# Early operand splits for the output projection, and twelve attention stages on other ticks

## The chip, the core and the metric

One core of one Trainium2 chip runs the whole program. The metric is the device time of one execution in microseconds. The kernel before took 687.49 us (median of three executions, from 686.54 to 687.96). The profiled execution took 686.53 us; its span from the first to the last instruction is 684.8 us. The clock that was granted to TensorE was 1.00 of full speed in the whole span.

The engines are called as in the profile: PE is TensorE's matmul, PEld its weight load, DVE is VectorE, ACT is ScalarE, POOL is GpSimd, SP is SyncE, which here only issues DMAs.

## What is computed

A layer normalisation feeds an attention with a compressive memory and a gated feed-forward network (FFN); both results are added to x. S is 2048, D is 448, there are 16 heads of 28 and 4 segments of 512 tokens, F is 1792.

```
xn = layernorm(x)
for each segment s of 512 tokens:                  # q, k, v = xn @ wq, xn @ wk, xn @ wv
    p = softmax(qs @ ks.T * scale + causal mask)   # within the segment, 16 heads
    a_dot = p @ vs
    a_mem = phi(qs) @ M / (phi(qs) @ z + 1e-6)     # M, z: sums over the earlier segments
    o[s] = g * a_mem + (1 - g) * a_dot
    M, z = M + phi(ks).T @ vs, z + sum(phi(ks))
out = x + o @ wo + (sigmoid(xn @ w_gate) * (xn @ w_up)) @ w_down
```

All matmul operands that need float32 accuracy are split in a high and a low part, and a product is made of eleven matmuls (the list `TERMS`): high by high, high by low and low by high.

## The kernel before

**Stages.** A front part (about the first 150 us) normalises x, and makes values, keys, queries and the memory's share, which goes to the DRAM tensors `od`. Then comes one long part with an order written out by hand, in which three streams of work are mixed; each engine works through its own instructions in the order in which the program gives them out.

1. The FFN (`gated`). For each of 7 pairs of feature tiles and each of 4 blocks of 512 tokens it makes two gate products and two up products of 11 matmuls each (line 254), and between them the down products of the block before, 6 matmuls each (line 180). ACT takes a tanh of a gate product (line 261), DVE multiplies it with the up product (line 271), ACT copies the result to `hh` (line 277), DVE makes its low part (line 280), and DVE adds each down product to `acc` (line 182). A block is 20 steps (`yield`s).
2. The attention within segments (`attention`). A `Pair` is two heads of a segment, a `Unit` two pairs, called A (even) and B (odd) here. There are 16 units.
3. The output projection (`project`): for each of 16 tiles of 128 tokens, `split_tokens` makes the high part of the attention's output in `xs` on ACT (line 802) and the low part on DVE (lines 109 and 110), and 11 matmuls (line 820) multiply it with the output weights. It begins when the FFN's generator is through; its first matmuls stand behind the splits of tiles 0, 1 and 2.

**Ticks.** The attention's work is put on a list of ticks, 28 to a unit (`TICKS`). After each step of the FFN or of the projection the main loop gives out as many ticks as are due, 473 ticks over 541 steps, so about 0.87 of a tick to a step. 28 ticks are 32 steps, so the units lie in five different ways on the FFN's blocks of 20 steps, and every fifth unit lies in the same way. Within a tick the work goes by rank: scores (0), exponents and the unit's sums (1), loads (2), maxima (3), joins (4), subtractions (5), the work behind a unit (6).

A pair goes through these stages; the tables give the tick of each, counted from the unit's first:

- `SCORES`, `score(k)`, five steps: PE makes a block of transposed scores (line 638) in one of two PSUM banks, ACT copies it to `w` (lines 642 and 645), POOL masks the diagonal (line 653). Step 0 takes a new buffer `w` of three; that buffer was the result's buffer of the unit two before, which a DMA of the POOL queue stores (line 740). After the last step SP issues the six loads of the pair after the next.
- `MAXIMA`, `maximum(k)`, three steps on DVE (lines 660 and 664): each needs the masked scores.
- `JOINS`, `join(k)`: step 0 is three small DVE maxima (lines 673 to 675) and a copy on POOL (678); step 1 is one DVE maximum (680) and a POOL copy (681); step 2 is one DVE maximum (683) and two POOL copies (684, 685); step 3 is a DVE transpose that spreads the maxima to `mb` (688).
- `SUBTRACT`, `subtract(k)`, three steps on DVE (line 702), and `EXPONENTS`, `exponents(k)`, three on ACT (line 706).
- At tick 28 + 15 `finish` makes the unit's sums (line 724) on PE out of the exponentials of both pairs.
- `BEHIND`: `back` (a DVE transpose out of PSUM, line 730), `divide` (142, 143), `turn` (736), and `store`, the DMA on the POOL queue.

PSUM has 8 banks: two for scores, two for up products, two shared by gate and down products, one for down products, one for the unit's sums. So a matmul waits for the DVE or ACT instruction that empties its bank, and `finish` for the exponentials.

`load_sums(0)` and `load_sums(1)` read the attention's output of the first two blocks back from DRAM; they are issued behind the last scores of pairs 30 and 31, at ticks 435 and 446.

Of the kernel before, what the change touches and what calls it, by code (L numbers as in the profile page):

```python
# [11 lines left out]
AF = mybir.ActivationFunctionType  # L12
# [4 lines left out]
P = 128  # L17
# [19 lines left out]


TICKS = 28
SCORES = ((2, 4, 7, 10, 15), (16, 20, 21, 24, 26))  # L40
MAXIMA = ((10, 13, 16), (23, 26, 28))
JOINS = ((17, 18, 19, 20), (29, 30, 31, 33))
SUBTRACT = ((22, 25, 26), (33, 34, 37))
EXPONENTS = ((25, 27, 31), (34, 36, 39))
BEHIND = (17, 18, 19, 24)
SUMS, END = 15, 25


# [20 lines left out]
def kernel(  # L69
# [11 lines left out]
    V, A, G, T = nc.vector, nc.scalar, nc.gpsimd, nc.tensor  # L81
# [6 lines left out]
    xs = [keep.tile([P, 7, L], F32R, name=f"xs{b}") for b in range(NB)]  # L88
# [18 lines left out]
    def transpose_low(p3, dst, t):  # L107
        tok = slice(t * P, (t + 1) * P)
        V.tensor_sub(dst[:, 4:7, tok], p3[:, 0:3], dst[:, 0:3, tok].bitcast(F32))
        V.tensor_sub(dst[64:, 3, tok], p3[64:, 3], dst[64:, 3, tok].bitcast(F32))  # L110
# [11 lines left out]
    def bank(name, tag):  # L122
        return ps.tile([P, L], F32, name=name, tag=tag, bufs=banks[tag])
# [177 lines left out]
    with tc.tile_pool(name="front", bufs=2) as sb, tc.manual_schedule(engines=FRONT):  # L301
# [227 lines left out]
        for b in range(NB):  # L529
# [24 lines left out]
            for k, c in enumerate((3, 4, 5, 6, 0, 1, 2) if last else range(7)):  # L554
# [34 lines left out]
                n = k - 1 if b == 0 else k + 1  # L589
# [152 lines left out]
    pairs = [Pair(n) for n in range(NB * H // 2)]  # L742
    units = [Unit(u, pairs[2 * u:2 * u + 2]) for u in range(NB * NG)]

    def attention():
        for n in range(2):
            pairs[n].load()
        units[0].load_values()
        yield
        plan = [[] for _ in range(n_att + 1)]  # L750

        def at(tick, rank, work, *args):
            plan[tick].append((rank, work, args))

        def following(n):
            if n < len(pairs):
                pairs[n].load()
            else:
                load_sums(n - len(pairs))

        for n, pair in enumerate(pairs):
            first = TICKS * (n // 2)
            ticks = [first + tick for tick in SCORES[n % 2]]
            for k, tick in enumerate(ticks):
                at(tick, 0, pair.score, k)
            at(ticks[-1], 2, following, n + 2)
            for k in range(3):
                at(first + MAXIMA[n % 2][k], 3, pair.maximum, k + 2)
                at(first + SUBTRACT[n % 2][k], 5, pair.subtract, k)
                at(first + EXPONENTS[n % 2][k], 1, pair.exponents, k)  # L770
            for k in range(4):
                at(first + JOINS[n % 2][k], 4, pair.join, k)
        for u, unit in enumerate(units):
            first = TICKS * (u + 1)
            at(first + SUMS, 1, unit.finish)
            if u + 1 < len(units):
                at(first + SUMS, 2, units[u + 1].load_values)
            for tick, work in zip(BEHIND, (unit.back, unit.divide, unit.turn, unit.store)):
                at(first + tick, 6, work)
        for work in plan:  # L780
            for _, run, args in sorted(work, key=lambda w: w[0]):
                run(*args)
            yield

    sums = {}

    def load_sums(b):

        if b < 2:
            sums[b] = sb.tile([P, HG, L], F32, name="sums", tag="qk2", bufs=2)  # L790
        else:
            sums[b] = sums[b - 2]
        o3 = od[b].rearrange("(h c) n -> h c n", c=32)
        for m in range(8):
            a, c = m % 2, 4 * min(m, 6)
            nc.sync.dma_start(sums[b][64 * a:64 * a + 64, m // 2, :], o3[:, c:c + 4, :])

    def project():

        def split_tokens(b, t):  # L800
            o3 = sums[b][:, :, t * P:(t + 1) * P]
            A.activation(xs[b][:, 0:4, t * P:(t + 1) * P], o3, AF.Copy)
            transpose_low(o3, xs[b], t)

        def out_weights(w):
            at = 2 * D * (w // 4) + D * (w % 2)
            return wo[w % 4 // 2][:, at:at + D]

        yield
        for n in range(NB * NT + 2):  # L810
            if n < NB * NT:
                b, t = divmod(n, NT)
                split_tokens(b, t)
                if t == NT - 1 and b + 2 < NB:
                    load_sums(b + 2)
            if n >= 2:
                b, t = divmod(n - 2, NT)
                po = bank("po", ("p", "gu")[n % 2])
                for m, (a, w) in enumerate(TERMS):
                    T.matmul(po[:, :D], xs[b][:, a, t * P:(t + 1) * P], out_weights(w),  # L820
                             start=m == 0, stop=m == len(TERMS) - 1)
                    if m in (3, 7):
                        yield
                halves = 2 if n == NB * NT + 1 else 1
                for i in range(halves):
                    part = slice(D // halves * i, D // halves * (i + 1))
                    V.tensor_add(acc[b][:, t, part], po[:, part], acc[b][:, t, part])
                    queue = nc.scalar if i else nc.sync
                    queue.dma_start(out[b * L + t * P:b * L + (t + 1) * P, part], acc[b][:, t, part])
                yield  # L830
                if rest:
                    yield from rest.pop(0)

    N_OUT = 1 + NB * NT * 3 + 12
    steps = attention()
    n_att = len(units) * TICKS + END
    done = 0
    with tc.manual_schedule(engines=MANUAL):
        next(steps)
        k = sum(FILLS) + 6  # L840
        for part in (ffn, project()):
            for _ in part:
                want = min(round(n_att * (k - LEAD) / (N_FFN + N_OUT - LEAD - TAIL)), n_att)
                k += 1
                while done < want:
                    next(steps)
                    done += 1
# [39 lines left out]
```

## Time and profile before

The program's parts in the profile, from the page's groups of instructions:

| group | instructions | busy us | mean ns |
|---|---|---|---|
| down products, PE line 180 | 672 | 155.3 | 366 |
| scores, PE line 638 | 256 | 62.0 | 314 |
| unit's sums, PE line 724 | 512 | 37.8 | 436 |
| output projection, PE line 820 | 176 | 36.7 | 364 |
| subtractions, DVE line 702 | 96 | 100.7 | 1055 |
| maxima, DVE line 660 | 64 | 79.0 | 1234 |
| additions of down products, DVE line 182 | 112 | 67.6 | 603 |
| exponentials, ACT line 706 | 96 | 87.9 | 916 |
| masks, POOL line 653 | 160 | 76.0 | 478 |

| | us |
|---|---|
| median of three executions | 687.49 |
| profiled execution | 686.53 |
| its span | 684.8 |

How to read the rows. A row of the timeline has the start (us from the span's start), the busy time, the engine, the line, the operation, out<-in, the shape, the number of instructions merged in it, and in brackets the time for which the engine sat idle before it with what ended that. A row of the waits has who waited for whom, the time in all, how often, and the longest. Matmuls overlap each other and their ends are modelled, so the starts tell more than the busy times.

### The profile page before, as it was taken

Reading aid. Unit: us, or ns where it says so; the run is one execution under the profiler, and the core shown is the slowest. Engines: PE = TensorE matmul, PEld = TensorE weight load, DVE = VectorE, ACT = ScalarE, POOL = GpSimd, SP = SyncE. Lnnn points to the kernel's source line nnn. Section 1 sums busy time; section 2 is a strip of 40 time slices with the busy share of each in tenths; the row PEclk is TensorE's granted clock in tenths of the full one; section 3 lists DMA queues with packets and bytes.
Section 4 is the critical chain, followed back from the end, with each engine's and each line's share of the span. In section 5 each row is a group of like instructions: output and inputs, shape, how many; then the busy total and the mean of one; then the engine's idle time right before and its main releaser. Section 6 shows DMA issues by size and latency. Waiting matters only on the chain.

```text
span 684.8 us, 10503 instructions
## 1 busy us (share of the span) xinstructions
PE 678.9 (99%) x3594; PEld 567.8 (83%) x3594; DVE 570.8 (83%) x995; ACT 338.6 (49%) x563; POOL 141.6 (21%) x349
## 2 busy tenths in 40 slices
PE   8999999999999999999999999999999999999998
PEld 7898878778878788887888878888787887888797
DVE  6765695766799899999999899899998998999754
ACT  5837555343364445645456455455544554544320
POOL 3500010101212232232212213132122231321000
PEclk9999999999999999999999999999999999999999
DMA  7446556696224331252324442324352332423352
GB/s 268 182 151 234 203 208 243 245 335 184 71 73 99 95 100 58 58 154 61 96 56 101 96 113 60 100 57 105 85 111 69 97 74 72 106 71 85 82 168 104
DMA packets 45940, 84.37 MB, mean 123 GB/s; under 512 B 6336, under 2 KB 20544, under 8 KB 45376
## 3 DMA queue, kind: packets, MB, share of 16 engines
q1 hardware_dynamic: 42736, 76.26, 37.0%
q0 software_dynamic: 3008, 7.34, 5.0%
q8 instruction: 28, 0.46, 0.3%
q14 instruction: 24, 0.20, 0.1%
q10 hardware_dynamic: 144, 0.11, 0.0%
HBM read 51.05 MB, written 32.64 MB: 122 GB/s over the span
## 4 chain that ended last, share of the span: by engine, by line
PE 89%; DVE 7%; issue 2%; POOL 1%; ACT 1%; DMA 0%; DVEq 0%; ACTq 0%; POOLq 0%
PE pgu L254 37%; PE pd L180 18%; PE pp L380 10%; PE st L638 5%; PE po L820 5%; PE pa L724 5%; PE pv L360 5%; PE pmm L408 2%; PE n L426 2%; DVE w L702 1%; DVE mx L660 1%; PE pt L102 1%; PE pk L400 1%; DVE acc L182 1%; DVE sg L271 0%
## 5 line engine op out<-in xcount | busy, mean ns | idle before, releaser
L254 PE MATMUL pgu<-xs,wgu 128*128 128x512 f32 x1232 | 302.6, 393 | 0.0
L254 PEld LDWEIGHTS pgu<-xs,wgu 128*128 128x128 f32 x1232 | 229.1, 188 | 46.2 <-issue 2.0
L180 PE MATMUL pd<-wdn,hh 128*128 128x448 f32 x672 | 155.3, 366 | 0.0
L180 PEld LDWEIGHTS pd<-wdn,hh 128*128 128x128 f32 x672 | 122.8, 188 | 11.5 <-issue 0.8
L653 POOL TENSOR_SCALAR_AFFINE_SELECT w<-w 128x256 f32<-128x256 f32 (+1 forms) x160 | 76.0, 478 | 231.2 <-ACT w L642 162.8
L706 ACT ACTIVATE w<-w 128x1024 f32<-128x1024 f32 (+1 forms) x96 | 87.9, 916 | 58.0 <-DVE w L702 58.0
L642 ACT ACTIVATE w<-st 128x512 f32<-128x512 f32 x128 | 75.7, 592 | 61.5 <-PE st L638 55.9
L702 DVE TENSOR_TENSOR w<-w,mb 128x1024 f32<-128x1024 f32 (+1 forms) x96 | 100.7, 1055 | 0.8
L660 DVE TRANSPOSE_TENSOR_REDUCE mx<-w 128x32 f32<-128x1024 f32 x64 | 79.0, 1234 | 6.6 <-POOL w L653 6.5
L380 PE MATMUL pp<-xs,wqk 128*128 128x512 f32 x308 | 77.7, 402 | 0.0
L182 DVE TENSOR_TENSOR acc<-pd,acc 128x448 f32<-128x448 f32 x112 | 67.6, 603 | 5.5 <-PE pd L180 5.5
L277 ACT ACTIVATE hh<-sg 128x512 fp32r<-128x512 f32 x56 | 35.4, 631 | 67.3 <-DVE sg L271 45.6
L380 PEld LDWEIGHTS pp<-xs,wqk 128*128 128x128 f32 x308 | 56.8, 188 | 13.4 <-issue 2.4
L638 PE MATMUL st<-qk 84*128 84x128 f32 (+3 forms) x256 | 62.0, 314 | 0.0
L261 ACT ACTIVATE sg<-pgu 128x512 f32<-128x512 f32 x56 | 33.2, 593 | 50.7 <-PE pgu L254 48.8
L638 PEld LDWEIGHTS st<-qk 84*128 84x128 f32 x256 | 47.9, 189 | 8.7 <-issue 1.4
L271 DVE SCALAR_TENSOR_TENSOR sg<-sg,pgu 128x512 f32<-128x512 f32 x56 | 37.8, 674 | 10.8 <-PE pgu L254 10.8
L387 DVE TENSOR_TENSOR qk<-pp,qk 128x512 fp32r<-128x512 f32 x28 | 19.3, 689 | 29.8 <-ACT e L385 23.7
L688 DVE STREAM_TRANSPOSE mb<-top 128x1024 f32<-128x1024 f32 x32 | 39.5, 1235 | 3.3 <-POOL top L685 3.2
L360 PE MATMUL pv<-wv,xs 128*128 128x448 f32 x176 | 39.6, 376 | 0.3 <-POOL wv L457 0.2
L280 DVE SCALAR_TENSOR_TENSOR hh<-sg,hh 128x512 fp32r<-128x512 f32 x56 | 38.2, 682 | 0.9 <-ACT hh L277 0.9
L724 PE MATMUL pa<-w,vv 128*32 128x128 f32 (+3 forms) x512 | 37.8, 436 | 0.0
(100 smaller groups left out, 638.5 us busy)
## 6 DMA issues: line engine op xcount, KB each, us to landing
qk<-qd SPq DMA_DIRECT2D x192, 112.0 KB
qd<-qk SPq DMA_DIRECT2D x28, 512.0 KB
raw<-in_w_ffn SPq DMA_DIRECT2D x14, 512.0 KB
vd<-vst SPq DMA_DIRECT2D x4, 1024.0 KB
vv<-vd SPq DMA_DIRECT2D x16, 256.0 KB
od<-w POOLq DMA_DIRECT2D x16, 256.0 KB, 4.2
sums<-od SPq DMA_DIRECT2D x32, 128.0 KB
out<-acc SPq DMA_DIRECT2D x15, 224.0 KB
```

The costliest lines, as they stand in the source:

```text
L180: T.matmul(pd[:, :D], l, r, start=n == 0, stop=n == len(mms) - 1)
L182: V.tensor_add(acc[b][:, t, :], pd[:, :D], acc[b][:, t, :])
L254: T.matmul(dst, wgu[f][:, w, side * P:(side + 1) * P], xs[b][:, a, :], start=n == 0, stop=n == len(TERMS) - 1)
L360: T.matmul(pv[:, :D], xs[b][:, a, t * P:(t + 1) * P], wv[w], start=n == 0, stop=n == len(TERMS) - 1)
L380: T.matmul(pp, wqk[c][:, w, :], xs[b][:, a, :], start=n == 0, stop=n == len(TERMS) - 1)
L638: T.matmul(st[:, at:at + L - kb * P], self.qk[:KS, 1, h, kb * P:(kb + 1) * P], self.qk[:KS, 0, h, kb * P:], start=True, stop=True)
L642: A.activation(w, st, AF.Copy)
L653: G.affine_select(d, d, pattern=pattern, base=0, channel_multiplier=-1, compare_op=ALU.is_ge, fill=MASK)
L660: V.tensor_reduce(self.mx[:, 32 * h:32 * h + 32], w3[:, h, :2 * L].rearrange("p (b n) -> p b n", n=32), axis=mybir.AxisListType.X, op=ALU. ...
L702: V.tensor_sub(w, w, m)
L706: A.activation(w, w, AF.Exp, scale=SCALE)
L724: T.matmul(pa[32 * j:32 * j + 32, kb * P:], self.vv[:, kb, 32 * j:32 * j + 32], self.pairs[j // 2].block(j % 2, kb), start=kb == 0, stop=k ...
```

## The change

Twelve entries of the tables get another tick, all but one of them a stage of pair A or of the work behind a unit. In pair A the first score moves from tick 2 to 0, the second maximum from 13 to 14 and the third from 16 to 17, the joins from 17, 18, 19, 20 to 18, 19, 20, 22, the last subtraction from 26 to 29 (tick 1 of the next unit) and the last exponential from 31 to 33 (tick 5). In pair B the first score moves from 16 to 17. Behind a unit, `divide` moves from 18 to 19 and `turn` from 19 to 20. `split_tokens` for tiles 0 and 1 of block 0 is given out at ticks 458 and 460, with rank 7, and no longer at the start of `project`.

```diff
-SCORES = ((2, 4, 7, 10, 15), (16, 20, 21, 24, 26))
-MAXIMA = ((10, 13, 16), (23, 26, 28))
-JOINS = ((17, 18, 19, 20), (29, 30, 31, 33))
-SUBTRACT = ((22, 25, 26), (33, 34, 37))
-EXPONENTS = ((25, 27, 31), (34, 36, 39))
-BEHIND = (17, 18, 19, 24)
+SCORES = ((0, 4, 7, 10, 15), (17, 20, 21, 24, 26))
+MAXIMA = ((10, 14, 17), (23, 26, 28))
+JOINS = ((18, 19, 20, 22), (29, 30, 31, 33))
+SUBTRACT = ((22, 25, 29), (33, 34, 37))
+EXPONENTS = ((25, 27, 33), (34, 36, 39))
+BEHIND = (17, 19, 20, 24)
+EARLY_SPLITS = (10, 12)
...
+    def split_tokens(b, t):
+        o3 = sums[b][:, :, t * P:(t + 1) * P]
+        A.activation(xs[b][:, 0:4, t * P:(t + 1) * P], o3, AF.Copy)
+        transpose_low(o3, xs[b], t)
...
+        for t in range(2):
+            at(TICKS * len(units) + EARLY_SPLITS[t], 7, split_tokens, 0, t)
...
-                split_tokens(b, t)
+                if n > 1:
+                    split_tokens(b, t)
```

The same function `split_tokens` stood in `project` before; it is moved so that both can call it.

More of the change, by code (lines that the diff above doesn't have):

```diff
@@ L798, in project @@
     def project():
[L800 to L803, printed above, removed]
         def out_weights(w):
```

## The prediction

> **What bounds the kernel now.** I read the page's totals first, then its two largest groups, then who waited for whom on the matmul engine and on DVE.
>
> ```profile
> span 684.8 us, 10503 instructions
> ...
> PE 678.9 (99%) x3594; PEld 567.8 (83%) x3594; DVE 570.8 (83%) x995; ACT 338.6 (49%) x563; POOL 141.6 (21%) x349
> ...
> DVE  6765695766799899999999899899998998999754
> ...
> L254 PE MATMUL pgu<-xs,wgu 128*128 128x512 f32 x1232 | 302.6, 393 | 0.0
> L254 PEld LDWEIGHTS pgu<-xs,wgu 128*128 128x128 f32 x1232 | 229.1, 188 | 46.2 <-issue 2.0
> ```
>
> ```profile
> PE po L820 <- DVE xs L109: 0.7, 1, 0.7
> ...
> PEld po L820 <- DVE xs L109: 1.0, 1, 1.0
> ...
> PEld st L638 <- ACT w L642: 0.4, 1, 0.4
> ...
> DVE sg L271 <- PE pgu L254: 10.8, 9, 2.7
> ...
> DVE mx L680 <- POOL up L678: 7.9, 11, 2.5
> DVE mx L660 <- POOL w L653: 6.5, 8, 2.3
> ...
> ACT w L642 <- DMA od<-w: 5.4, 3, 2.6
> ```
>
> PE is busy in 99% of the span. A busy PE alone proves little, since ends are modelled; but from about 155 us on the only waits of PE or PEld for another engine of over 0.2 us are the two quoted: the projection's matmul for DVE's split, once, and a score for ACT's copy, once. So TensorE sets the time, and the change can win those two waits and no more: about one microsecond. DVE is the second engine: in the attention's part nearly every slice has a 9, and what idle time it has (10.8, 7.9 and 6.5 us in the quoted waits, over 16 units) is about 1.6 us a unit. It runs some microseconds behind PE, and PE does not feel that as long as the results that it needs are early enough. The question is what twelve moved stages do to that lead.
>
> **Part 1, the early splits.** The place is where the unit's sums end and the projection begins.
>
> ```profile
> 632.32 0.69 DVE L702 TENSOR_TENSOR w<-w,mb 128x512 f32<-128x512 f32 x1
> ...
> 633.10 0.64 ACT L706 ACTIVATE w<-w 128x512 f32<-128x512 f32 x1 [0.37 <-DVE w L702]
> ...
> 635.50 2.36 PE L724 MATMUL pa<-w,vv 128*32 128x512 f32 x32
> ...
> 636.87 4.26 ACT L802 ACTIVATE xs<-sums 128x512 fp32r<-128x512 f32 x8
> ...
> 637.79 0.68 PE L820 MATMUL po<-wo,xs 128*128 128x448 f32 x2
> ...
> 638.57 0.52 DVE L109 TENSOR_TENSOR xs<-sums,xs 128x384 fp32r<-128x384 f32 x1
> 639.11 0.29 DVE L110 TENSOR_TENSOR xs<-sums,xs 64x128 fp32r<-64x128 f32 x1
> 639.13 1.71 PEld L820 LDWEIGHTS po<-wo,xs 128*128 128x128 f32 x9 [1.05 <-DVE xs L109]
> 639.13 2.08 PE L820 MATMUL po<-wo,xs 128*128 128x448 f32 x9 [0.67 <-DVE xs L109]
> ```
>
> The first two matmuls need only the high part; the third, with the low part, stands until DVE's line 109 is done at 639.09. PE's modelled idle time is 0.67 us, that of the weight loads 1.05; I take 0.85, between them. From the third matmul on there is no wait to the end, so this comes off the end in full.
>
> With the change the two splits are given out at ticks 458 and 460, before the unit's sums (tick 463). On ACT they cost 4.26 / 8 = 0.53 us each, on DVE 0.52 + 0.29 = 0.81 each. On ACT the first stands ahead of the last exponential (633.10) and delays it by at most 0.53 us, to about 634.3; the sums begin at 635.50, so over a microsecond of cover is left. On DVE they take 1.6 us of a stretch after the last subtraction, in which it idles for a part; what is queued behind them there (the split of the second half of the output weights, an FFN product, `back`) has its matmuls after 639. The third split stays where it is and its tile comes two tiles later. The work is moved, not added: the cost is 0, or 0.5 us if that cover were gone.
>
> **Part 2, the score at tick 0.** PE's score and ACT's copy of it come two ticks earlier, about 2 us (473 ticks over some 485 us). The copy still has to wait for the buffer that the store frees (the 5.4 us of ACT in the quoted waits), so ACT will stand at that place for up to 2 us longer. Behind it in ACT's queue stand an `hh` copy or a tanh, and in POOL's queue, behind the mask, the copy of B's join 0. The loads of its operands were issued 13 ticks before instead of 15. It ends the one wait of a score for a copy: 0.44 us on PEld at most, 0 if the store is as late as the copy; I take 0.2.
>
> **Part 3, the maximum at tick 17 and the joins.** This is where I expect the loss. Every fifth unit lies in the same way on the FFN's steps; I show one, and take the two others of its kind to be like it.
>
> ```profile
> 552.02 1.48 PE L180 MATMUL pd<-wdn,hh 128*128 128x448 f32 x6
> 552.29 1.23 DVE L660 TRANSPOSE_TENSOR_REDUCE mx<-w 128x32 f32<-128x1024 f32 x1
> ...
> 553.53 0.62 DVE L182 TENSOR_TENSOR acc<-pd,acc 128x448 f32<-128x448 f32 x1
> 553.57 2.67 PE L254 MATMUL pgu<-xs,wgu 128*128 128x512 f32 x11
> ...
> 554.08 0.17 DVE L673 TENSOR_TENSOR mx<-mx 128x24 f32<-128x24 f32 x1
> ...
> 554.48 0.18 DVE L675 TENSOR_TENSOR mx<-mx 128x16 f32<-128x16 f32 x1
> ...
> 554.58 0.71 DVE L730 STREAM_TRANSPOSE w<-pa 128x512 f32<-128x512 f32 x1
> ...
> 556.27 0.69 DVE L271 SCALAR_TENSOR_TENSOR sg<-sg,pgu 128x512 f32<-128x512 f32 x1 [0.98 <-PE pgu L254]
> ...
> 556.88 0.18 DVE L680 TENSOR_TENSOR mx<-mx,up 64x32 f32<-64x32 f32 x1
> ```
>
> ```profile
> 540.90 0.18 DVE L680 TENSOR_TENSOR mx<-mx,up 64x32 f32<-64x32 f32 x1 [0.37 <-POOL up L678]
> ```
>
> Line 271 waits for the up product, whose end PE sets. Before, DVE did the maximum, join 0 and `back` ahead of it, and join 1 could follow at once, since POOL had its copy done. By the ticks the order becomes: addition, maximum, `back`, line 271, join 0, join 1. So join 0 (554.08 to 554.66, 0.58 us) falls behind the wait, and join 1 then waits for POOL with nothing between, 0.37 us as at 540.90. DVE comes out 0.95 us later; 0.58 if the copy is hidden. After that it works without a pause worth the name up to these rows:
>
> ```profile
> 575.67 0.62 DVE L182 TENSOR_TENSOR acc<-pd,acc 128x448 f32<-128x448 f32 x1
> ...
> 576.83 1.37 PE L180 MATMUL pd<-wdn,hh 128*128 128x448 f32 x6
> ...
> 578.10 0.63 ACT L706 ACTIVATE w<-w 128x512 f32<-128x512 f32 x1
> ...
> 578.36 2.36 PE L724 MATMUL pa<-w,vv 128*32 128x512 f32 x32
> ...
> 579.25 0.13 PEld L724 LDWEIGHTS pa<-w,vv 128*32 128x32 f32 x4 [0.30 <-issue]
> ```
>
> The down product at 576.83 needs the bank that line 182 empties by 576.29: 0.54 us of lead, against 0.58 to 0.95 us of delay, so PE stands for 0.04 to 0.41 us. Then the last exponential, which ends at 578.73, feeds the sums' second block, which begins near 579.25: some 0.4 us of lead are left, and the delay takes 0 to 0.15 more. That is 0.04 to 0.55 a unit; I take 0.4, near the upper end, since no row shows the copy hidden when nothing stands between. Three units: 1.2 us.
>
> ```profile
> 292.43 1.22 DVE L660 TRANSPOSE_TENSOR_REDUCE mx<-w 128x32 f32<-128x1024 f32 x1
> 295.17 0.69 DVE L271 SCALAR_TENSOR_TENSOR sg<-sg,pgu 128x512 f32<-128x512 f32 x1 [1.53 <-PE pgu L254]
> ```
>
> Once more, in the unit at 292, the maximum itself changes places with line 271: 1.22 us of work goes behind a wait of 1.53 us, and with join 1's 0.37 DVE is 1.6 us late there. What lead the next sums have I bound by 0.4 us from the rows above and the whole 1.6 us: a loss of 0 to 1.2, taken at 0.4, because half a unit of DVE's waits lies between and can absorb some.
>
> ```profile
> 608.09 0.63 ACT L706 ACTIVATE w<-w 128x512 f32<-128x512 f32 x1
> ...
> 608.18 1.07 PE L724 MATMUL pa<-w,vv 128*32 128x512 f32 x8
> ```
>
> In the units at 436 and 580 the maximum already stood behind line 271, and only join 1's 0.37 us is new. At the sums that follow the exponential ends at 608.72, 0.54 us after they began; by the distance of 0.89 us to the second block (578.36 to 579.25) 0.35 us of lead are left, less a weight load of 0.13. So 0 to 0.2 a unit; I take 0.15, 0.3 for both.
>
> **Part 4, the rest.** A's last subtraction goes between B's joins 0 and 1 and fills the 0.37 us for which DVE waited there: 0 to 0.37 gained on DVE, which PE feels only where a lead is short; counted 0. The last exponential at tick 33 has a lead of ten ticks to the sums; B's first score, a tick later, has three ticks to the score that needs its bank; `divide` and `turn` come a tick later, four ticks ahead of the store: 0, and if ACT's queue is late there, some 0.1 each time.
>
> **The sum.** 686.53 - 0.85 - 0.2 + 1.2 + 0.4 + 0.3 = 687.38 us against the profiled execution, +0.85 us. That execution is the fastest that is shown, 0.96 us below the median; on the median the same step gives 687.49 + 0.85 = 688.34, said as **688.3 us**. A measurement of this kernel can tell about 0.2% (1.37 us) from no change, so this is no change that can be told.
>
> **Rivals.**
>
> *DVE has no lead to give (slower).* If the delays at tick 17 pass to PE whole, because DVE's idle places of about 1.6 us a unit are used up and one unit's delay reaches the next, the three units cost 0.95 each, the one at 292 1.6, the two others 0.37 each, and a late store under the score at tick 0 some 0.3 once: 5.5 us. With the gains of 1.05 that is +4.4 at most; half of the excess over my sum gives the likely size, +2.6: 690.1 us. It decides from the point where the delay is larger than the leads of 0.2 to 0.54 us that the rows show. For it: those leads are short. Against: the subtraction in the joins' gap gives back up to 0.37 a unit.
>
> *Only the gains.* The moved stages cost PE nothing: 687.49 - 1.05 = 686.4 us. For it: DVE's waits on POOL (7.9 and 6.5 us) are at just the stages that now get more room. Against: the order above, in which work goes behind a wait.
>
> *PE has room that its busy time hides (faster).* ACT's 5.4 us behind the store may be felt by PE under the modelled ends; if a quarter of it went with the moves, 1.4 us, the time would be 687.49 - 1.05 - 1.4 = 685.0. Against: eleven matmuls with 2.67 us from first start to last end (553.57) are as even as their loads. The Trainium skill speaks for it: Perfetto Trace Analysis, Identifying the Most-Contended Engine, says that matmul busy time misleads and that weight-load busy time tells the distance to the limit, which here is 83%. The trace does not agree that this is room: a load takes 188 ns, the wait behind it is not for another engine, and 46.2 us of PEld's idle time at line 254 has 2.0 us with a named end.
>
> *The early splits are not early*, since the third matmul then waits for something else, say the split of the output weights that they delay: part 1 is worth 0, and the sum 689.2.
>
> **Chances.** My sum 0.40, DVE without a lead 0.38, only the gains 0.12, hidden room 0.06, splits not early 0.04. Of the first, 0.34 lies within 0.2%, 0.04 above and 0.02 below; of the gains alone 0.08 within and 0.04 below; the slower rival lies above but for 0.02; the last is half and half. That makes faster 0.12, the same 0.46, slower 0.42. The range goes from the gains alone to a little past the slower rival: 686.3 to 690.5.
>
> **What would show it.** Right: the third matmul of line 820 follows the second without a wait on line 109; no score waits for line 642; DVE's join 0 stands behind line 271 at the places like 556, and a down product or the sums get a short wait for DVE or ACT about 15 to 20 us later. Wrong: PE's waits for other engines in the attention stay nil (then only the gains count), or they appear in most units (then the first rival). The forecast as a whole is wrong below 686.1 or above 688.9, 0.2% from the median.

## The result, and the profile after

| kernel | median us | lowest to highest | ratio to before, 95% interval |
|---|---|---|---|
| before | 687.05 | 686.54 to 687.96 (7 runs) | |
| changed | 689.49 | 687.93 to 690.79 (7 runs) | 1.0033 (1.0023 to 1.0043) |

The change makes the kernel 2.44 us slower, 0.33%, a little more than the 0.2% that a measurement can tell. The spread is twice as wide as well, 2.9 us against 1.4. The profiled execution of the changed kernel took 690.79 us, the longest of the seven, and that of before 686.53, the shortest, so the two traces differ by 4.26 us, more than the medians do. Which part of that is steady has to come from the experiments.

From the page of the changed kernel, the span and the engines' totals:

```profile
span 689.0 us, 10521 instructions
...
PE 679.0 (99%) x3594; PEld 566.2 (82%) x3594; DVE 570.0 (83%) x995; ACT 339.1 (49%) x563; POOL 153.8 (22%) x349
```

No engine is busy for over 0.5 us longer than before but GpSimd (141.6 before), and PE is again busy for 99%. The 4.2 us are in the waits. From the view of who waited for whom (us in total, times, longest):

```profile
ACT w L643 <- DMA od<-w: 18.7, 10, 4.7
...
PE st L639 <- ACT w L643: 2.3, 2, 1.3
PE pd L181 <- DVE acc L183: 1.7, 3, 0.6
```

The line numbers of the attention and the FFN are one higher than before (line 182 is now 183, 638 is 639, 642 is 643). The wait of the projection for DVE's split is gone. Two kinds of wait of PE are new: three down products wait for DVE's addition, and two scores for ACT's copy; ACT in turn waits for the store's DMA, 18.7 us where it was 5.4.

What each wait costs shows better in the distance between the starts of neighbouring groups of matmuls than in PE's modelled idle time. PE's rows of the timeline, before:

```profile
394.51 2.67 PE L254 MATMUL pgu<-xs,wgu 128*128 128x512 f32 x11
397.21 0.51 PE L638 MATMUL st<-qk 84*128 84x256 f32 x2
...
538.93 2.68 PE L254 MATMUL pgu<-xs,wgu 128*128 128x512 f32 x11
541.45 0.40 PE L638 MATMUL st<-qk 84*128 84x256 f32 x2
...
574.24 2.75 PE L254 MATMUL pgu<-xs,wgu 128*128 128x512 f32 x11
```

and after:

```profile
285.72 2.75 PE L255 MATMUL pgu<-xs,wgu 128*128 128x512 f32 x11
288.90 1.28 PE L181 MATMUL pd<-wdn,hh 128*128 128x448 f32 x5 [0.43 <-DVE acc L183]
...
395.30 2.68 PE L255 MATMUL pgu<-xs,wgu 128*128 128x512 f32 x11
399.32 0.50 PE L639 MATMUL st<-qk 84*128 84x256 f32 x2 [1.33 <-ACT w L643]
...
432.19 2.75 PE L255 MATMUL pgu<-xs,wgu 128*128 128x512 f32 x11
435.57 1.48 PE L181 MATMUL pd<-wdn,hh 128*128 128x448 f32 x6 [0.63 <-DVE acc L183]
...
541.98 2.68 PE L255 MATMUL pgu<-xs,wgu 128*128 128x512 f32 x11
545.66 0.50 PE L639 MATMUL st<-qk 84*128 84x256 f32 x2 [1.00 <-ACT w L643]
...
578.53 2.75 PE L255 MATMUL pgu<-xs,wgu 128*128 128x512 f32 x11
581.90 1.27 PE L181 MATMUL pd<-wdn,hh 128*128 128x448 f32 x5 [0.62 <-DVE acc L183]
...
640.69 2.36 PE L725 MATMUL pa<-w,vv 128*32 128x512 f32 x32
...
642.98 2.48 PE L824 MATMUL po<-wo,xs 128*128 128x448 f32 x11
```

The undisturbed distance to the down product is 576.83 - 574.24 = 2.59 us. After, it is 3.18, 3.38 and 3.37: the three waits cost 0.59, 0.79 and 0.78, 2.16 us together. The scores come 4.02 and 3.68 us behind the group ahead of them, where before they came 2.70 and 2.52: 1.32 and 1.16, 2.48 us together. From the last sums to the end of the span it is 689.0 - 640.69 = 48.3 us, and before 684.8 - 635.50 = 49.3: 1.0 gained, with the projection's first eleven matmuls in one group at 642.98. That gives 2.16 + 2.48 - 1.0 = 3.6 of the 4.2 us; the rest lies in differences of about 0.1 us that I can't place.

### The profile page after: what moved, and what is told of

It reads as the page before. It is cut to its first block, busy times and chain, and to the rows that moved or that the text cites. A ratio compares the mean times of both kernels' runs of the same rounds, so it can differ in the third digit from the quotient of the medians.

```text
span 689.0 us, 10521 instructions
## 1 busy us (share of the span) xinstructions
PE 679.0 (99%) x3594; PEld 566.2 (82%) x3594; DVE 570.0 (83%) x995; ACT 339.1 (49%) x563; POOL 153.8 (22%) x349
## 4 chain that ended last, share of the span: by engine, by line
PE 85%; DVE 8%; DMA 3%; issue 2%; POOL 1%; ACT 0%; SPq 0%; DVEq 0%; POOLq 0%; ACTq 0%
PE pgu L255 34%; PE pd L181 17%; PE pp L381 10%; PE pa L725 5%; PE po L824 5%; PE st L639 5%; PE pv L361 5%; DMA od<-w 2%; DVE w L703 2%; PE pmm L409 2%; PE n L427 1%; DVE mb L689 1%; DVE mx L661 1%; DMA acc<-in_x 1%; PE pt L103 1%
## 5 line engine op out<-in xcount | busy, mean ns | idle before, releaser
L654 POOL TENSOR_SCALAR_AFFINE_SELECT w<-w 128x256 f32<-128x256 f32 (+1 forms) x160 | 83.3, 520 | 284.1 <-ACT w L643 214.8
L725 PE MATMUL pa<-w,vv 128*32 128x128 f32 (+3 forms) x512 | 37.8, 436 | 0.0
```

The costliest lines, as they stand in the source:

```text
L654: G.affine_select(d, d, pattern=pattern, base=0, channel_multiplier=-1, compare_op=ALU.is_ge, fill=MASK)
L725: T.matmul(pa[32 * j:32 * j + 32, kb * P:], self.vv[:, kb, 32 * j:32 * j + 32], self.pairs[j // 2].block(j % 2, kb), start=kb == 0, stop=k ...
```

## Where DVE gets late

DVE's rows of the timeline of the changed kernel, at the unit that the prediction took as its example:

```profile
557.84 0.62 DVE L183 TENSOR_TENSOR acc<-pd,acc 128x448 f32<-128x448 f32 x1 [1.00 <-PE pd L181]
558.38 1.23 DVE L661 TRANSPOSE_TENSOR_REDUCE mx<-w 128x32 f32<-128x1024 f32 x1
...
560.59 0.69 DVE L272 SCALAR_TENSOR_TENSOR sg<-sg,pgu 128x512 f32<-128x512 f32 x1 [0.38 <-PE pgu L255]
561.20 0.18 DVE L674 TENSOR_TENSOR mx<-mx 128x24 f32<-128x24 f32 x1
...
562.15 0.18 DVE L681 TENSOR_TENSOR mx<-mx,up 64x32 f32<-64x32 f32 x1 [0.37 <-POOL up L679]
...
566.87 0.89 DVE L281 SCALAR_TENSOR_TENSOR hh<-sg,hh 128x512 fp32r<-128x512 f32 x1
...
581.23 0.62 DVE L183 TENSOR_TENSOR acc<-pd,acc 128x448 f32<-128x448 f32 x1
```

This is the order that was forecast: addition, maximum, `back`, the multiply of line 272 (old 271), join 0, and join 1 after 0.37 us of standing. From the multiply's start to join 1 it is 1.56 us (562.15 - 560.59), before 0.61 (556.88 - 556.27): 0.95 us, as the prediction worked out. What it did not see is that the delay grows: the addition of line 183 ends at 581.85, 3.32 us after the group of eleven at 578.53 began, against 2.05 before (576.29 - 574.24). So DVE is 1.27 us late there.

Some 0.2 us of the growth is line 281, 0.89 us for a mean of 0.68 before. GpSimd's row at that time:

```profile
566.03 1.19 POOL L654 TENSOR_SCALAR_AFFINE_SELECT w<-w 128x256 f32<-128x256 f32 x1 [1.54 <-ACT w L643]
```

A mask of 128x256 took 0.41 us at 564.08 in this trace, and 0.62 in the mean. Here it begins inside the subtraction of line 703 (565.72 to 566.94) and ends 0.3 us after it, inside line 281. The Trainium skill has a rule for this (SBUF — State Buffer, Who interferes with whom): a DVE instruction with two inputs in SBUF contends with a GpSimd instruction that reads SBUF, since the ports that the two engines share are locked by one of them at a time. Both rows agree with it. They are no proof, since spans on GpSimd are rough.

## The experiments

Those named "with a tile of its own" replace one line of `finish` by two, so that a unit's result does not lie in a tile that a later pair's scores are copied into, and no copy has to wait for the store:

```diff
-            self.on, self.oc = (self.pairs[1].w[:, n * L:(n + 1) * L] for n in range(2))
+            self.on = self.pairs[1].w[:, 0:L]
+            self.oc = sb.tile([P, L], F32, name="oc")
```

Each group of runs below is from one chip, and the kernel before ran beside it: 686.73, 686.65 and 686.67 us in the first, second and third group, and 686.60 beside the last run. These agree within 0.13 us, so medians are compared across the groups too.

| run | median us | lowest to highest | ratio to before, 95% interval |
|---|---|---|---|
| early splits alone | 685.76 | 685.47 to 686.13 | 0.9983 (0.9974 to 0.9991) |
| A's joins, third maximum and `BEHIND` back | 685.79 | 685.33 to 687.87 | 0.9988 (0.9979 to 0.9997) |
| scores back | 690.07 | 688.45 to 691.42 | 1.0043 (1.0029 to 1.0057) |
| changed, own tile | 688.02 | 687.72 to 688.43 | 1.0015 (1.0006 to 1.0023) |
| own tile, joins back | 686.47 | 686.40 to 686.83 | 0.9997 (0.9988 to 1.0006) |
| own tile, maximum and `BEHIND` back | 686.90 | 686.73 to 687.37 | 1.0003 (0.9994 to 1.0011) |
| before, own tile | 686.61 | 686.39 to 686.87 | 0.9996 (0.9987 to 1.0005) |
| early splits alone, own tile | 685.66 | 685.32 to 686.02 | 0.9983 (0.9975 to 0.9992) |
| changed, store at 22 | 688.00 | 687.84 to 688.35 | 1.0019 (1.0009 to 1.0028) |
| changed, once more | 689.73 | 688.33 to 690.16 | 1.0042 (1.0029 to 1.0055) |
| own tile, division between joins 0 and 1 | 687.93 | 687.78 to 688.20 | 1.0019 (1.0010 to 1.0028) |
| early splits, store at 22 | 685.69 | 685.53 to 686.07 | 0.9985 (0.9976 to 0.9994) |

**First group: which part of the change costs.** The early splits alone have all six tables of before:

```diff
-SCORES = ((0, 4, 7, 10, 15), (17, 20, 21, 24, 26))
-MAXIMA = ((10, 14, 17), (23, 26, 28))
-JOINS = ((18, 19, 20, 22), (29, 30, 31, 33))
-SUBTRACT = ((22, 25, 29), (33, 34, 37))
-EXPONENTS = ((25, 27, 33), (34, 36, 39))
-BEHIND = (17, 19, 20, 24)
+SCORES = ((2, 4, 7, 10, 15), (16, 20, 21, 24, 26))
+MAXIMA = ((10, 13, 16), (23, 26, 28))
+JOINS = ((17, 18, 19, 20), (29, 30, 31, 33))
+SUBTRACT = ((22, 25, 26), (33, 34, 37))
+EXPONENTS = ((25, 27, 31), (34, 36, 39))
+BEHIND = (17, 18, 19, 24)
```

> The early splits alone, with all ticks of before. If the splits do what the change says, the one wait of the projection's third matmul goes and nothing else changes: 0.8 to 1.0 us faster than before (ratio 0.9987), no wait of a matmul of line 824 for line 110. If the two splits only push other work of ACT and DVE behind them (the rival), the time is that of before within 0.3 us, and another wait stands near the projection's start.

Measured: 685.76, 0.97 us below before, with the eleven matmuls of the projection now in one group without a wait:

```profile
638.15 2.48 PE L824 MATMUL po<-wo,xs 128*128 128x448 f32 x11
```

So the early splits bring what they should, and the moved stages take it back, and more.

The second run undoes three of the tables:

```diff
-MAXIMA = ((10, 14, 17), (23, 26, 28))
-JOINS = ((18, 19, 20, 22), (29, 30, 31, 33))
+MAXIMA = ((10, 13, 16), (23, 26, 28))
+JOINS = ((17, 18, 19, 20), (29, 30, 31, 33))
-BEHIND = (17, 19, 20, 24)
+BEHIND = (17, 18, 19, 24)
```

> The changed kernel with pair A's maxima and joins and the two stages behind a unit back on their old ticks; scores, last subtraction, last exponential and early splits stay moved. Theory 1 (join 0 behind the FFN's product on DVE makes DVE about 1 us late in every fifth unit): the three waits of a down product for line 183 (1.7 us on PE, 2.2 us by the starts) go, and the kernel is about 2.2 us faster than the changed one. The rival (the moved score at tick 0 makes DVE late, through POOL's queue): the three waits stay.

Measured: 685.79, level with the early splits alone, and 3.7 us below the changed kernel where the theory had 2.2: the three waits for line 183 went, and in the median the loss by the store went with them. So the score at tick 0, B's first score at 17 and A's last subtraction and exponential at 29 and 33 cost and win nothing in the median. It shows more: this kernel has the score at tick 0, and its ACT stands longer for the store than in any other:

```profile
ACT w L643 <- DMA od<-w: 19.4, 11, 4.4
...
PE st L639 <- ACT w L643: 1.0, 1, 1.0
```

19.4 us of standing on ACT came to one wait of 1.0 us on PE in the profiled execution, and to nothing in the median. Not all executions are free of it: three of the twelve, the profiled one among them, took 686.72 to 687.87.

The third takes the scores back instead:

```diff
-SCORES = ((0, 4, 7, 10, 15), (17, 20, 21, 24, 26))
+SCORES = ((2, 4, 7, 10, 15), (16, 20, 21, 24, 26))
```

> The changed kernel with the two scores back on ticks 2 and 16, all else moved. Theory 2 (the first score two ticks earlier puts ACT behind the store's landing, and a score at tick 7 pays for it): the two waits of a score for ACT's copy (2.7 us by the starts) shrink to the 0.2 us of before, and the three waits for line 183 stay: about 1 us faster than the changed one by the median. The rival (the landing of the store alone decides, and varies from run to run whatever the tick): the waits for the copy come and go as in the changed kernel, and the medians are equal within 0.5 us.

Measured: 690.07, not faster than the changed kernel. ACT's standing for the store falls to 10.6 us, and PE's two waits stay:

```profile
ACT w L643 <- DMA od<-w: 10.6, 6, 2.1
...
PE st L639 <- ACT w L643: 2.6, 2, 1.4
```

The tick of the first score is not what makes the score of tick 7 wait.

The fourth is the changed kernel with a tile of its own.

> The changed kernel, with the unit's result turned into a tile of its own instead of the third buffer w, so that no score's copy waits for the store. If the landing of the store is what a score at tick 7 pays for, ACT has no wait for the DMA od<-w (18.7 us in the changed kernel), the two waits of a score for the copy go, the three waits for line 183 stay, and the runs lie closer together: about 1 us faster than the changed one by the median, near 688.3. If ACT's wait for the store is covered (rival), nothing changes.

Measured: 688.02, within 0.7 us from lowest to highest. Both waits for line 643 are gone, and the three for line 183 stay. So the changed kernel has two separate losses: a steady one, and one that comes and goes with the store.

**Second group: what makes the steady loss.** On the kernel with a tile of its own, first A's joins alone go back:

```diff
-JOINS = ((18, 19, 20, 22), (29, 30, 31, 33))
+JOINS = ((17, 18, 19, 20), (29, 30, 31, 33))
```

> The changed kernel with the result in a tile of its own, so that no copy waits for the store, and with A's joins alone back at ticks 17 to 20; the third maximum stays at 17 and the turn at 20. Theory 1 (join 0 behind the multiply at line 272 makes DVE about 1 us late, and three down products wait for line 183, 2.2 us together): the three waits go and the time is 685.7 to 686.2 us, some 2.1 below the same kernel with the joins at 18 to 22 (688.02). Theory 2 (the maximum at 17, or the turn and the division a tick later, make DVE late): at least half of the 2.2 us stays, 687.0 or more, with waits of line 181 for line 183.

then everything of the three tables but the joins:

```diff
-MAXIMA = ((10, 14, 17), (23, 26, 28))
+MAXIMA = ((10, 13, 16), (23, 26, 28))
-BEHIND = (17, 19, 20, 24)
+BEHIND = (17, 18, 19, 24)
```

> The changed kernel with the result in a tile of its own, and with the third maximum back at 16 and division and turn back at 18 and 19; A's joins stay at 18, 19, 20 and 22. Theory 1 (the place of join 0 decides): the three waits of line 181 for line 183 stay at 0.5 to 0.8 us each, and the time is 687.6 to 688.2 us. Theory 2 (maximum, division and turn decide): the waits go, 685.7 to 686.5.

Against these stand the kernel before and the early splits alone, both with a tile of its own:

> The kernel before with the result in a tile of its own, and nothing else. If the waiting for the store's landing costs the kernel before only in some executions, its median falls by 0 to 0.3 us, to 686.4 to 686.7, and its spread to under 0.8 us. If that wait were a steady part of the time, it falls by 0.5 or more. Either way the score's wait of 0.18 us at 397 goes.

> The kernel before with the early splits and with the result in a tile of its own. If the two gains are independent, it is 0.95 below the kernel before with a tile of its own, and 0 to 0.3 below the early splits alone (685.76): 685.4 to 685.8 us, with a spread under 0.8.

Neither account of the steady loss held. From the base of 685.66 us (early splits, own tile, tables of before), maximum and `BEHIND` cost 686.47 - 685.66 = 0.81 us, the joins 686.90 - 685.66 = 1.24, and both together 688.02 - 685.66 = 2.36. Each of the two sets alone makes DVE late enough. The group of eleven, the addition and the down product in the timelines of the base, of the kernel with the joins back, and of that with maximum and `BEHIND` back:

```profile
574.23 2.75 PE L255 MATMUL pgu<-xs,wgu 128*128 128x512 f32 x11
575.66 0.62 DVE L183 TENSOR_TENSOR acc<-pd,acc 128x448 f32<-128x448 f32 x1
576.81 0.37 PE L181 MATMUL pd<-wdn,hh 128*128 128x448 f32 x1
```

```profile
574.72 2.75 PE L255 MATMUL pgu<-xs,wgu 128*128 128x512 f32 x11
576.97 0.62 DVE L183 TENSOR_TENSOR acc<-pd,acc 128x448 f32<-128x448 f32 x1
...
577.64 1.48 PE L181 MATMUL pd<-wdn,hh 128*128 128x448 f32 x6 [0.17 <-DVE acc L183]
```

```profile
574.95 2.75 PE L255 MATMUL pgu<-xs,wgu 128*128 128x512 f32 x11
577.32 0.62 DVE L183 TENSOR_TENSOR acc<-pd,acc 128x448 f32<-128x448 f32 x1
...
578.00 1.27 PE L181 MATMUL pd<-wdn,hh 128*128 128x448 f32 x5 [0.30 <-DVE acc L183]
```

Counted from the group's start, the addition ends at 2.05, 2.87 and 2.99 us, and in the changed kernel at 3.32: DVE is 0, 0.82, 0.94 and 1.27 us late. The down product starts at 2.58, 2.92, 3.05 and 3.37: it is 0, 0.34, 0.47 and 0.79 us late. The wait is the delay less 0.47 or 0.48 us each time. That is the lead; whatever DVE loses beyond it, PE loses too, at up to three places in the run.

What the maximum does to DVE shows in its timeline with the joins back:

```profile
554.04 0.62 DVE L183 TENSOR_TENSOR acc<-pd,acc 128x448 f32<-128x448 f32 x1 [2.50 <-PE pd L181]
554.58 1.23 DVE L661 TRANSPOSE_TENSOR_REDUCE mx<-w 128x32 f32<-128x1024 f32 x1
...
558.03 0.18 DVE L684 TENSOR_TENSOR top<-mx,up 32x32 f32<-32x32 f32 x1 [0.29 <-POOL up L682]
```

DVE stands for 2.50 us ahead of the addition, whose operand PE has not made yet. Before, the maximum was done in that time; now it comes behind it. The idle time has moved from a place behind the maximum, where the multiply waited 0.98 us, to one ahead of it. The multiply, at 557.00 and without a wait, now starts 2.92 us after its group of eleven (554.08), where in the base it was 2.71 (556.26 - 553.55): 0.21 us late. Then join 2 stands for 0.29 us for GpSimd's copy, since the division, which stood ahead of it in the base, is behind it at tick 19, and line 281 takes 0.89 us here too, 0.68 in the base. These three make 0.71 of the 0.82 us. The maximum was not moved without the division and the turn, so what it costs by itself is not shown.

The two others held in their times. The kernel before gains 0.04 us from a tile of its own (686.65 to 686.61) and the early splits 0.95 beside it (686.61 to 685.66). One thing that was expected did not come: with a tile of its own the score at 397 waits as before, 0.45 us on the weight load, so that wait is not one for the store.

**Third group: the store, and join 1's standing.** Theory: the score of tick 7 waits because the copy that frees its bank waits for the store, and the store lands late. It is moved two ticks ahead in the changed kernel, with nothing else:

```diff
-BEHIND = (17, 19, 20, 24)
+BEHIND = (17, 19, 20, 22)
```

> The changed kernel with the store of a unit's result at tick 22 instead of 24, about 2 us earlier; all else as changed. Theory (the store lands too late, 6.6 to 7.0 us after its issue, for the score of tick 7): the score's waits of 1.49 and 1.16 us for line 643 go, the three waits for line 183 (2.2 us) stay, and the time is 687.8 to 688.4 us, as with a tile of its own, with a spread under 1. Rival (the store ends only when the loads issued about it end, so its landing does not move): the two waits stay at over 0.5 us each, and the time is 689.0 to 690.1.

> The changed kernel as it is, on the chip of the two others, as their measure. If the landing of the store differs from execution to execution, it has a spread of 1.5 us or more and a median of 688.5 to 690.0; in its profile the three waits for line 183 are 2.1 to 2.3 us together as before, and the score's waits for line 643 come out at another size than 2.65 us. If the landing were a fixed part of the schedule, they are again 2.6 to 2.7 us and the spread is under 1.

Measured: 688.00, within 0.5 us from lowest to highest, as with a tile of its own, against 689.73 of the changed kernel on the same chip. Here is the first of the two places in the changed kernel, with the store, the loads on SP's queue and ACT's copies:

```profile
390.04 2.48 SPq L621 DMA_DIRECT2D qk<-qd  x6
...
391.63 0.86 POOL L741 DMA_DIRECT2D od<-w  x1
...
392.62 0.36 SPq L192 DMA_DIRECT2D raw<-in_w_ffn  x1
...
398.67 0.60 ACT L643 ACTIVATE w<-st 128x512 f32<-128x512 f32 x1 [4.74 <-DMA od<-w]
```

and in the kernel with the earlier store:

```profile
387.77 0.86 POOL L741 DMA_DIRECT2D od<-w  x1
...
390.12 2.48 SPq L621 DMA_DIRECT2D qk<-qd  x6
...
393.93 0.58 ACT L643 ACTIVATE w<-st 128x512 f32<-128x512 f32 x1
```

The views of the DMA give the landing. In the changed kernel from 380 to 402 us, one store; with the earlier store from 330 to 630 us, the median of eleven; KB each, and us from issue to landing:

```profile
od<-w POOLq DMA_DIRECT2D x1, 256.0 KB, 7.0
```

```profile
od<-w POOLq DMA_DIRECT2D x11, 256.0 KB, 4.0
```

The store was issued amid 6 x 112 KB of loads, with the 512 KB of the weights right behind, and took 7.0 us. Ahead of them it takes 4.1 here and 4.0 in the median, and the copy, at 393.93 there, no longer waits. The gain in issue is 3.9 us against the loads, not two ticks, since the store now also stands ahead of a mask in GpSimd's queue. The kernel before agrees, from 330 us on: its four stores that were issued 1.3 us or more ahead of the loads (at 360, 447, 505 and 591 us) landed in 3.9 to 4.2 us, and the two that were issued 1.2 and 1.6 us behind them in 5.7 and 4.9.

How late the score comes follows from the landing. With the store at 22 it starts 2.52 us after its group of eleven (397.91 - 395.39). In the changed kernel it is 4.02, 1.50 more with a landing of 7.0 us; in the kernel with A's joins, third maximum and `BEHIND` back 1.12 more with one of 6.6; in the changed kernel run once more 0.26 more with one of 5.7. Each time that is the landing less some 5.5 us.

The changed kernel once more came out at 689.73 and with the same three waits for line 183, while its scores waited 1.1 us by PE's modelled idle time where the first profile has 2.3. So the store's landing differs between executions of one kernel, and PE sees it only when it comes later than those 5.5 us.

The last of the group tests the 0.37 us for which join 1 stands, on the changed kernel with a tile of its own. The division is put there:

```diff
-JOINS = ((18, 19, 20, 22), (29, 30, 31, 33))
+JOINS = ((18, 20, 21, 22), (29, 30, 31, 33))
```

> The changed kernel with the result in a tile of its own, and A's joins at 18, 20, 21 and 22, so that DVE's division (line 144) stands between join 0 and join 1 while GpSimd copies. Theory (DVE's delay of 1.27 us at line 183 holds 0.37 us of standing for that copy): the standing goes, the three waits for line 183 fall by 0.3 to 0.4 us each, from 0.61, 0.79 and 0.79 to about 0.25, 0.42 and 0.42, and the time is 686.8 to 687.1 us. Rival (the later joins 1 and 2 make the mask's transposition as late as before): the waits stay over 0.55 each and the time is 687.7 to 688.3.

Measured: 687.93 where it was 688.02. The three waits are 0.47, 0.67 and 0.82 us by the starts, where they were 0.60, 0.78 and 0.79. By the time the rival held, though it put all three waits over 0.55:

```profile
561.66 1.25 DVE L689 STREAM_TRANSPOSE mb<-top 128x1024 f32<-128x1024 f32 x1 [0.46 <-POOL top L686]
```

Join 1 waits no more, and join 3 waits 0.46 us for GpSimd instead. The joins are a chain that goes from DVE to GpSimd and back three times; here, what was filled at the first crossing opened at the last.

**A version that beats both.** The early splits with the store at 22 and the other tables of before:

> The kernel before with the early splits and with the store at tick 22. If the early splits give their 0.95 us here too and the earlier store lands in some 4 us, clear of the score of tick 7, the time is 685.4 to 685.8 us (the early splits alone: 685.76), with a spread under 0.8 us and no wait of the score at 397. If the earlier store takes room from the masks and copies that follow it on GpSimd, waits of DVE for GpSimd grow and the time is over 686.0.

Measured: 685.69. It is 0.9 us below before, and no better than the early splits alone (685.76): with those tables the store lands in time for the score in most executions anyway. The score at 397 still waits, which was not expected; the next section comes back to it.

## Why the prediction came out as it did

It said 688.3 us, or 0.85 above the median of the three executions of before that were known (687.49), and held no measurable change for the likeliest (0.46) and slower for almost as likely (0.42). The measurement is 689.49, 2.44 above before: inside the range, but slower by more than can be called no change, and above the 688.9 from which the prediction calls itself wrong. Of its four signs three came: the projection's third matmul without a wait, join 0 behind the multiply, and short waits of down products some 20 us later. The fourth, that no score waits for ACT's copy, did not.

- **The early splits, -0.85:** right, in size and in cause. 0.95 to 0.97 us in the runs.
- **The score at tick 0, -0.2:** in the median it brought nothing and cost nothing (685.79 with it, 685.76 without). That ACT would stand longer was right (5.4 to 18.7 us), and the quoted wait of 0.4 us on the weight load does end with it: the score then starts 2.52 us after its group, where before it was 2.70. But that wait was never one for the store. It is there in the last kernel of the experiments, in which the store is issued at 386.55 and lands in 4.0 us:

```profile
396.15 0.63 ACT L278 ACTIVATE hh<-sg 128x512 fp32r<-128x512 f32 x1 [2.91 <-DVE mx L674]
...
397.32 0.30 PEld L639 LDWEIGHTS st<-qk 84*128 84x128 f32 x2 [0.44 <-ACT w L643]
```

  Ahead of the score's copy, at 396.69, ACT works on an `hh` copy, and that one waits for DVE. The step that failed is the landing of the store: part 2 let ACT stand for it and put that at nothing for PE, and the sum had no term for it. In the slower rival it stood at "some 0.3 once", with the quoted execution's landing of 4.9 us. It takes up to 7.0, 1.5 more than the lead, and the two scores came 2.48 us later in the profile; in the medians the difference between the changed kernel and that with the earlier store is 1.7 us (689.73 - 688.00). The tick of the first score does not decide it, since the loss stays with the scores back.
- **The three units, +1.2:** the right places (288.90, 435.57, 581.90), the right engine and the right wait, with the size at half: 0.59, 0.79 and 0.78 us where 0.4 was taken. The first delay was as worked out, 0.95 us. The step that failed here is "after that it works without a pause", which took the delay as constant: it grew to 1.27 us at line 183. The lead was 0.48 where the rows gave 0.54, since the down product starts 0.05 us after the addition ends. And join 0 is not the only cause: the maximum at tick 17, which was written down as part of the order but not costed, costs 0.81 us with the joins back in their places, together with the division and the turn, which part 4 put at 0.
- **The unit at 292, +0.4, and those at 436 and 580, +0.3:** they did not occur. No sums wait on PE; their 512 matmuls are as busy as before, 37.8 us, with no idle time:

```profile
L725 PE MATMUL pa<-w,vv 128*32 128x128 f32 (+3 forms) x512 | 37.8, 436 | 0.0
```

The lead of the sums was worked out from the weight loads of their second block. Such loads did wait for ACT (1.2 us in all, five times), but no matmul stood for it.

- **The sum:** without the store it would have been 2.36 - 0.95 = 1.41 us; the forecast's 0.85 comes near only because 0.7 us for the sums, which was too much, stands against 1.2 too little for the three units (2.36 for 1.2). That is luck, not the mechanism. With the store's wait the loss is 2.4 to 3.1 us.
- **The rivals:** the slower one has the nearest time, 690.1, but not the mechanism: the delays do not pass to PE whole, they pass less 0.48 us, at three places and not in six units. "Only the gains" is what the early splits do when they stand alone. Hidden room was not found: the early splits alone gain the wait that they remove and nothing besides. That the splits are not early fell with the first run.

What stays open is why the store lands late in most executions of the kernels whose DVE is late. It is issued 1.6 us after the loads in both (391.63 - 390.04, and 390.84 - 389.26 before), and landed at that place in 4.9 us before, in 4.7 with the early splits alone, in 7.0 after, in 5.7 when the changed kernel was run once more, and in 6.6 in the profiled execution with A's joins, third maximum and `BEHIND` back, whose DVE is not late. That it lands sooner when it is issued ahead of the loads is shown; what tips it from one execution to the next is not. The kernels with the DVE delay waited for it in the median, those without only in some executions, and no run explains that.

## What to carry to other kernels

In a schedule written out by hand, list for each moved stage not its own slack but that of the next result that the bound engine takes from the same queue: a delay costs nothing up to that lead and in full beyond it. Where a result that the bound engine needs stands behind a transfer, do not take the landing of one profile as its time: ask what the latest landing would do, and issue the transfer ahead of the loads that it competes with. Before a small wait is counted as a gain, follow it back one step further than the engine that it names. Work that used to fill an engine's wait is not free to move, even where another wait lies a few instructions on.

## What the hardware showed beyond that

- A 256 KB store from GpSimd's queue took 4.0 us (median of eleven) when issued ahead of SP's loads, and 4.7 to 7.0 at one and the same place among about 1.2 MB of them.
- ACT's 19.4 us of standing in the kernel with the joins back cost nothing in the median; in the changed kernel, 18.7 us went with a loss. The sum of an engine's waits says little; the row in which the bound engine waits for it says more.
- A mask on GpSimd, 0.62 us in the mean, took 1.19 beside a DVE subtraction, and the DVE instruction behind that took 0.89 us for a mean of 0.68.
